# Two transposing transfers joined into one, and a planned order replaced by a written one, in an attention and feed-forward kernel

## The chip, the cores and the metric

The kernel runs on one core of a Trainium2 chip. A core has five engines that run side by side: PE (matrix products), DVE, ACT and POOL (element-wise work and copies) and SP, which here issues nearly all transfers. Each engine takes its instructions strictly in order and waits at an instruction until the semaphores that it names have been raised. The metric is the time of one execution on the device in microseconds (us). Before the change three runs gave 361.81, 362.72 and 363.73 us, a median of 362.72 us. One more execution was profiled; it took 361.35 us, and its trace spans 359.6 us from the first to the last instruction.

## The reference

There are 8 batches of 8 heads, 576 positions and a head size of 64. Each head has two attentions: one over positions pooled by four (144 of them), and one in a band of 7 positions around each query. Their sum, with the heads laid side by side (512 values for each of 4608 tokens), goes through a gated feed-forward.

```
q_d = q.reshape(B, H, Sd, factor, D).mean(axis=3)      # k_d and v_d likewise, factor = 4
out_up = np.repeat(sm_attn(q_d, k_d, v_d), factor, axis=2)
mask = np.abs(pos[:, None] - pos[None, :]) < factor
scores = np.where(mask, scale * np.matmul(q, k.transpose(0, 1, 3, 2)), -1000000000.0)
out_local = np.matmul(softmax(scores), v)
x = (out_up + out_local).transpose(0, 2, 1, 3).reshape(4608, 512)
out = (np.maximum(x @ w_gate, 0.0) * (x @ w_val)) @ w_out      # 512 -> 1536 -> 512
```

## The kernel before

**Pairs.** Two heads make a pair; there are 32 pairs, four for each batch. The work of pair p is a set of named operations that end in p. `lq`/`lk` load q and k. `cast` turns them into 16-bit values in the tile `c16`. The transposition puts the 64 features on partitions: for pairs 0 to 7 it is done on PE (`T`), from pair 8 on by a transposing transfer that SP issues (`dT`, line 1487), which reads 9 blocks of 128 x 128 from `c16` (`c` in the profile) and writes `tq`. `ev` copies `tq` into `qkT`, `pl` (DVE, line 1507) pools it, and `S` on PE makes the band scores (line 1518) and the pooled scores (line 1530). The band goes through `msk`, `mx`, `sub`, `exp`, `sm`, `rc`, `nrm` and two 32 x 32 transpositions on DVE (`tr0`, `tr1`). The pooled scores go through `dmx` (line 1592), `nb` (line 1595), three exponentials `exd0` to `exd2` (ACT, line 1605), `rcd` (line 1627) and `nrd` (POOL, line 1631) into the tile `wd`; then they too must be transposed: on PE (`W`) for pairs 0 to 7, and from pair 8 on by a second transposing transfer (`dW`, line 1654), 6 blocks from `wd` into `wT`. `V` on PE (lines 1731 and 1739) multiplies both by v. `od` (ACT) and `xa0`, `xa1` (DVE) add the two parts into the tile `xT`. Most tiles of a pair have three copies, used in turn by p mod 3.

**Feed-forward.** The tokens are taken in steps of mostly 512. `hg` and `hv` are the gate and value products (line 1798), 12 of each for a step; `rl` (ACT, line 1812) takes the positive part of the gate, and `gm` (DVE, line 1819) multiplies it by the value into `gT`. `y` is the output product of one block of 128 tokens (line 1864), in three parts of four matmuls; block 35, the last, has two halves of 256 columns (`y35_0`, `y35_1`, line 1843). ACT copies each block to an output buffer (`yc`, line 1873, and line 1851 for block 35) and SP stores it (`st`, line 1881, and 1854).

**Output buffers.** There are two, `y_sb` 0 and 1, each of two blocks. Blocks 28 and 29 take buffer 0, 30 and 31 buffer 1, 32 and 33 buffer 0, 34 and 35 buffer 1. Up to block 31 one store of 512 KB takes both blocks; blocks 32 to 34 are stored one by one (256 KB), and block 35 in two stores of 128 KB. A copy into a buffer waits until the store that last read this buffer has landed.

**Order.** A planner (`list_schedule`) gives every operation an estimated start, from estimated durations, priorities and a table of shifts by name (`RANKS`), chooses the engine where several can do it, and writes the operations out in that order. Ahead of a PE operation it also puts filler products of zeros (`emit_zeros`, line 1360, 128x512 each) where it foresees an idle PE in the first 34 us: 41 of them, beside 12 at the very start.

Of the kernel before, what the change touches and what calls it, by code (L numbers as in the profile page):

```python
# [21 lines left out]
class Op:  # L22
# [4 lines left out]
    def __init__(self, eng, dur, emit, deps=(), prio=0.0, need=None, key=None, free=(),  # L27
# [14 lines left out]
SEM = 0.12  # L42

MARGIN = 0.0


LATE, LATE_V = 0.0, 0.0
FETCH, FETCH_LATE, BUSY = 4.5, 4.0, 80.0

DMA_START = {SP: 0.8, POOL: 2.2}  # L50
RECEIPT = 1.2
W_AT = (14.0, 30.0, 34.0, 38.0)
WO_T0, WO_DT = 52.0, 6.0

# [3 lines left out]

FILL = 34.0
STOP = 0.3  # L60
LQ = (1.0, 1.3)
ISSUE = 0.75

RANKS = {
    -1054.5: (
        "lv2_25 "
    ),
    -699.5: (
        "od8 "
    ),  # L70
    -689: (
        "pl3 "
    ),
    -668.5: (
        "exd2_8 "
    ),
    -661: (
        "sub8 "
    ),
    -660: (  # L80
        "vd8 "
    ),
    -624: (
        "msk25 "
    ),
    -598.5: (
        "nb8 "
    ),
    -597: (
        "lv2_2 "  # L90
    ),
    -586: (
        "rc8 "
    ),
    -572: (
        "lq8 "
    ),
    -559.5: (
        "lv2_8 "
    ),  # L100
    -559: (
        "lk8 cast8 ev8 pl8 mx8 exd0_8 exd1_8 nrm8 nrd8 lv0_8 lv1_8 lv3_8 vc8 VP8 V8 xa0_8 "
        "xa1_8 "
    ),
    -558: (
        "msk8 "
    ),
    -548: (
        "rcd8 "
    ),  # L110
    -540.5: (
        "nb27 "
    ),
    -532: (
        "cast5 lv1_11 "
    ),
    -525: (
        "dT8 "
    ),
    -524: (  # L120
        "rc4 "
    ),
    -523.5: (
        "mx26 "
    ),
    -509: (
        "sm8 "
    ),
    -489: (
        "cast3 "  # L130
    ),
    -480: (
        "lv2_28 "
    ),
    -479.5: (
        "lv0_28 lv1_28 lv3_28 "
    ),
    -474: (
        "vs28 "
    ),  # L140
    -468: (
        "dW8 "
    ),
    -460.5: (
        "lv3_0 "
    ),
    -449: (
        "msk11 "
    ),
    -413: (  # L150
        "lv3_5 "
    ),
    -401.5: (
        "vd23 "
    ),
    -395.5: (
        "dmx7 "
    ),
    -372.5: (
        "cast26 "  # L160
    ),
    -364: (
        "od28 "
    ),
    -356.5: (
        "dT23 "
    ),
    -356: (
        "sub0 sub1 sub2 sub3 "
    ),  # L170
    -351: (
        "vd27 "
    ),
    -349.5: (
        "ev30 "
    ),
    -347.5: (
        "lv2_5 "
    ),
    -347: (  # L180
        "lv0_5 lv1_5 "
    ),
    -339: (
        "rcd9 "
    ),
    -338.5: (
        "sm7 "
    ),
    -338: (
        "nb11 "  # L190
    ),
    -333: (
        "exd2_28 "
    ),
    -325.5: (
        "sub28 "
    ),
    -324.5: (
        "vd28 "
    ),  # L200
    -322: (
        "dmx25 "
    ),
    -319.5: (
        "msk6 "
    ),
    -310.5: (
        "od0 od1 od2 od3 "
    ),
    -299: (  # L210
        "exp8 "
    ),
    -291: (
        "msk26 "
    ),
    -279: (
        "S8 "
    ),
    -271.5: (
        "vs15 "  # L220
    ),
    -265.5: (
        "vs23 "
    ),
    -263: (
        "nb28 "
    ),
    -254.5: (
        "lq0 "
    ),  # L230
    -251: (
        "mx30 "
    ),
    -250.5: (
        "rc28 "
    ),
    -249.5: (
        "exp12 "
    ),
    -249: (  # L240
        "msk12 "
    ),
    -247.5: (
        "nrd11 "
    ),
    -244.5: (
        "cast21 "
    ),
    -243: (
        "msk18 "  # L250
    ),
    -236.5: (
        "lq28 "
    ),
    -234: (
        "l4_28 "
    ),
    -233.5: (
        "dmx28 "
    ),  # L260
    -233: (
        "exp11 "
    ),
    -223.5: (
        "lk28 cast28 ev28 pl28 mx28 exp28 exd0_28 exd1_28 nrm28 nrd28 vc28 V28 xa0_28 "
        "xa1_28 "
    ),
    -221: (
        "ev11 "
    ),  # L270
    -220.5: (
        "exp9 "
    ),
    -212.5: (
        "rcd28 "
    ),
    -191: (
        "pl11 "
    ),
    -190: (  # L280
        "sub11 "
    ),
    -189.5: (
        "dT28 "
    ),
    -184.5: (
        "exd2_1 "
    ),
    -181: (
        "od23 "  # L290
    ),
    -176.5: (
        "exd2_5 od25 "
    ),
    -175: (
        "exd0_1 "
    ),
    -173.5: (
        "sm28 "
    ),  # L300
    -173: (
        "sm4 od26 "
    ),
    -169.5: (
        "od13 "
    ),
    -168: (
        "lv3_26 "
    ),
    -160.5: (  # L310
        "lv1_26 "
    ),
    -150: (
        "exd2_23 "
    ),
    -146.5: (
        "exd2_29 "
    ),
    -145.5: (
        "exd2_25 "  # L320
    ),
    -142.5: (
        "sub23 "
    ),
    -142: (
        "exd2_26 "
    ),
    -140.5: (
        "od9 od10 od11 od12 od14 od15 od16 od17 od19 od20 od21 od22 od24 od27 od29 od30 "
    ),  # L330
    -138.5: (
        "exd2_13 "
    ),
    -138: (
        "sub25 "
    ),
    -137: (
        "vd25 "
    ),
    -134.5: (  # L340
        "sub26 "
    ),
    -133.5: (
        "vd26 "
    ),
    -132.5: (
        "dW28 "
    ),
    -130: (
        "xa1_0 xa1_2 xa1_3 vd13 xa0_16 xa1_16 "  # L350
    ),
    -117.5: (
        "msk14 "
    ),
    -117: (
        "rc19 "
    ),
    -113: (
        "ev0_2 "
    ),  # L360
    -111: (
        "dmx20 "
    ),
    -110: (
        "dmx10 "
    ),
    -109.5: (
        "exd2_0 exd2_2 exd2_3 exd2_9 exd2_10 exd2_11 exd2_12 exd2_14 exd2_15 exd2_16 "
        "exd2_17 exd2_18 exd2_20 exd2_21 exd2_22 exd2_24 exd2_27 exd2_30 "
    ),  # L370
    -107: (
        "vd5 "
    ),
    -103: (
        "pl21 "
    ),
    -102: (
        "sub9 sub10 sub12 sub14 sub16 sub17 sub18 sub19 sub22 sub24 sub27 sub30 "
    ),
    -101.5: (  # L380
        "lv2_24 "
    ),
    -101: (
        "vd9 vd10 vd11 vd12 vd14 vd15 vd16 vd17 vd18 vd19 vd20 vd21 vd22 lv0_24 lv1_24 vd24 "
        "vd29 vd30 "
    ),
    -100.5: (
        "lk2 exd1_11 "
    ),
    -100: (  # L390
        "exd0_0 exd0_3 msk16 pl27 "
    ),
    -99.5: (
        "lq30 "
    ),
    -97.5: (
        "od5 "
    ),
    -96: (
        "nb18 "  # L400
    ),
    -94: (
        "rc5 "
    ),
    -88.5: (
        "lk0 "
    ),
    -87.5: (
        "nrd18 "
    ),  # L410
    -85: (
        "rcd0 rcd1 rcd2 "
    ),
    -80: (
        "nb23 "
    ),
    -75.5: (
        "nb25 "
    ),
    -75: (  # L420
        "exd1_1 "
    ),
    -72: (
        "nb26 "
    ),
    -71: (
        "mx18 "
    ),
    -70.5: (
        "xa1_23 "  # L430
    ),
    -69: (
        "msk20 "
    ),
    -68.5: (
        "nb13 "
    ),
    -68: (
        "lv3_24 "
    ),  # L440
    -67.5: (
# [1522 lines left out]
```

## Time and profile before

| what | value |
|---|---|
| median of three runs | 362.72 us |
| the profiled execution's own time | 361.35 us |
| its span | 359.6 us |
| busy time of PE, DVE, POOL and ACT | 350.2, 247.9, 204.5 and 202.8 us |
| granted PE clock, mean over the span | 0.999 |
| moved by transfers | 64.80 MB, 180 GB/s |

The busy time of an engine is the time in which at least one of its instructions runs; PE's instructions overlap, so this alone does not say that PE works at its peak. The chain of waits follows the work that ended last back to its cause at each step. A wait is time in which an engine stood still, with the instruction that released it.

### The profile page before, as it was taken

To read this page: it belongs to the slowest core of one execution; us is meant where nothing else is said; L and a number is where in the kernel's file an instruction comes from. 1 tells how busy PE (TensorE), PEld (TensorE's weight loads), DVE (VectorE), ACT (ScalarE), POOL (GpSimd) and SP (SyncE) were. 2 spreads that over 40 slices of the span, in tenths; PEclk is the share of its full clock that TensorE was granted. 3 is DMA by queue.
4 is the path that set the end of the run, shared out by engine and by line. 5 is a ranking of instruction groups with operands and counts; after the bars stand their busy time and mean duration, and the time that the engine had idled before them with its cause. 6 is when DMAs were issued, how large, how long until landed. Compare 5 with 4: busy or idle time off the path is not lost.

```text
span 359.6 us, 10503 instructions
## 1 busy us (share of the span) xinstructions
PE 350.2 (97%) x4241; PEld 182.5 (51%) x4241; DVE 247.9 (69%) x477; ACT 202.8 (56%) x481; POOL 204.5 (57%) x240
## 2 busy tenths in 40 slices
PE   7988999999999999999999999999999999999996
PEld 3554556445545554555555454544555454445554
DVE  4666998717988898978895986788988853223210
ACT  2477786537874757664566485768654533233222
POOL 7798475933387888684986369476898400000000
PEclk9999999999999999999999999999999999999999
DMA  7999999779999999999999898999994220011022
GB/s 190 201 272 255 195 227 292 110 185 152 259 232 212 228 280 167 278 224 264 198 230 233 190 271 182 215 261 224 217 237 65 47 93 26 0 60 59 0 75 102
DMA packets 122067, 64.80 MB, mean 180 GB/s; under 512 B 100386, under 2 KB 106402, under 8 KB 122018
## 3 DMA queue, kind: packets, MB, share of 16 engines
q1 hardware_dynamic: 116194, 59.41, 75.7%
q0 software_dynamic: 5824, 4.72, 8.6%
q8 instruction: 33, 0.54, 0.7%
q14 instruction: 16, 0.13, 0.1%
HBM read 47.59 MB, written 9.44 MB: 159 GB/s over the span
## 4 chain that ended last, share of the span: by engine, by line
PE 90%; POOL 5%; DMA 1%; issue 1%; DVE 1%; ACT 1%; POOLq 0%; SPq 0%
PE bank L1798 52%; PE bank L1864 25%; PE bank L1518 4%; PE bank L1731 2%; PE bank L1739 2%; DMA gT<-in_q_dram 1%; PE bank L1530 1%; POOL wo_sb L1330 1%; PE bank L1640 1%; PE bank L1695 1%; POOL vw L1352 1%; POOL wd L1631 1%; PE bank L1843 1%; POOL vw L1330 1%; POOL e L1615 1%
## 5 line engine op out<-in xcount | busy, mean ns | idle before, releaser
L1819 DVE TENSOR_TENSOR gT<-r,bank 128x512 f16<-128x512 f16 (+1 forms) x112 | 74.6, 666 | 64.1 <-PE bank L1798 59.9
L1798 PE MATMUL bank<-xT,wg_sb 128*128 128x512 f16 (+2 forms) x528 | 112.2, 341 | 0.0
L1798 PE MATMUL bank<-xT,wv_sb 128*128 128x512 f16 (+2 forms) x528 | 112.2, 341 | 0.0
L1812 ACT ACTIVATE r<-bank 128x512 f16<-128x512 f32 (+1 forms) x112 | 65.1, 583 | 67.2 <-PE bank L1798 62.9
L1864 PE MATMUL bank<-wo_sb,gT 128*128 128x512 f16 x420 | 96.6, 379 | 0.0
L1798 PEld LDWEIGHTS <-wg_sb 128*128 128x128 f16 x528 | 44.2, 98 | 45.5 <-issue 0.4
L1798 PEld LDWEIGHTS <-wv_sb 128*128 128x128 f16 x528 | 44.2, 98 | 44.6 <-issue 0.6
L1864 PEld LDWEIGHTS <-gT 128*128 128x128 f16 x420 | 39.8, 98 | 44.6 <-issue 0.4
L1873 ACT COPY y_sb<-bank 128x512 f32<-128x512 f32 x35 | 20.5, 586 | 52.0 <-PE bank L1864 49.6
L1330 POOL CAST vw<-vw 128x1536 f16<-128x1536 f32 x28 | 40.9, 1461 | 2.7 <-DMA vw<-in_v_dram 1.9
L1507 DVE TENSOR_REDUCE qkd<-qkT 128x288 f16<-128x1152 f16 x28 | 37.5, 1340 | 3.7 <-ACT qkT L1329 3.5
L1586 POOL TENSOR_TENSOR s_sb<-s_sb,mx 128x384 f32<-128x384 f32 x28 | 23.2, 831 | 28.8 <-DVE mx L1583 27.9
L1605 ACT ACTIVATE wd<-bank,nmb 128x144 f16<-128x144 f32 x96 | 35.6, 381 | 4.3 <-POOL nmb L1595 3.1
L1621 DVE STREAM_TRANSPOSE at<-e 64x384 f16<-64x384 f16 x64 | 36.4, 569 | 1.6 <-POOL e L1615 0.9
L1615 POOL TENSOR_TENSOR e<-e,rs 128x384 f16<-128x384 f16 x32 | 26.8, 839 | 14.7 <-DVE rs L1613 11.3
L1631 POOL TENSOR_TENSOR wd<-wd,rsd 128x432 f16<-128x432 f16 x32 | 29.0, 908 | 8.7 <-DVE rsd L1627 6.8
L1759 DVE TENSOR_TENSOR xT<-bank,od_sb 128x288 f16<-128x288 f32 (+2 forms) x68 | 26.7, 430 | 9.9 <-ACT od_sb L1750 9.8
L1717 POOL TENSOR_TENSOR vs<-v 104x512 f32<-104x512 f32 x20 | 25.3, 1267 | 2.1 <-DMA v<-in_v_dram 1.9
L1329 ACT COPY qkT<-tq 128x1152 f16<-128x1152 f16 x21 | 25.3, 1205 | 1.5 <-DMA tq<-c 1.4
L1518 PEld LDWEIGHTS <-qkT 64*32 64x32 f16 x1536 | 17.2, 90 | 11.9 <-issue 7.3
L1518 PE MATMUL bank<-qkT 64*32 64x32 f16 x1536 | 20.6, 180 | 1.0 <-DVE xT L1759 0.7
L1330 POOL CAST c<-qk 128x1152 f16<-128x1152 f32 x16 | 18.2, 1147 | 5.3 <-issue 3.9
(67 smaller groups left out, 347.5 us busy)
## 6 DMA issues: line engine op xcount, KB each, us to landing
vw<-in_v_dram SPq DMA_DIRECT2D x126, 96.0 KB, 4.7
out_dram<-y_sb SPq DMA_DIRECT2D x16, 512.0 KB, 3.8
qk<-in_q_dram SPq DMA_DIRECT2D x14, 576.0 KB, 4.9
qk<-in_k_dram SPq DMA_DIRECT2D x14, 576.0 KB, 6.9
v<-in_v_dram SPq DMA_DIRECT2D x10, 640.0 KB, 7.4
wv_sb<-in_moe_w_val_dram POOLq DMA_DIRECT2D x4, 384.0 KB, 10.0
wg_sb<-in_moe_w_gate_dram POOLq DMA_DIRECT2D x4, 384.0 KB, 9.4
wo_sb<-in_moe_w_out_dram POOLq DMA_DIRECT2D x4, 384.0 KB, 8.3
```

The costliest lines, as they stand in the source:

```text
L1330: return lambda o: engine[eng].tensor_copy(out=dst, in_=src(o))
L1507: nc.vector.tensor_reduce(out=qkd[S3].rearrange("p (x t) -> p x t", x=2), in_=qk_sums, axis=AX.X, op=ALU.add)
L1518: nc.tensor.matmul(out=scv[32 * c : 32 * c + 32, i, :], lhsT=cols(hh, q0 + step * 24 * blk, 32), rhs=cols(hh, k0 + step * (24 * blk - 3), 32),
L1605: exd.append(add(ACT, 0.37, lambda o, i=i: nc.scalar.activation(out=_sap(wd_, 0, 128, 256 * i + K0, kd_cols), in_=_sap(dview()[:, i, :], 0 ...
L1615: r["nrm"] = nrm = add_any(either(lambda o, e: e.tensor_tensor(out=e_, in0=e_, in1=bc12(rs[S3]), op=ALU.mult), (POOL, 0.84), (DVE, 0.5)), ...
L1621: tr.append(add(DVE, 0.575, lambda o, lo=lo: nc.vector.transpose(out=at2[S3][lo : lo + 64, :, lo // 2 : lo // 2 + 32], in_=e_[lo : lo + 64 ...
L1631: r["nrd"] = nrd = add_any(either(lambda o, e: e.tensor_tensor(out=_sap(wd_, 0, 128, K0, w3), in0=_sap(wd_, 0, 128, K0, w3), in1=_sap(rsd[ ...
L1759: nc.vector.tensor_tensor(out=xT[:, kk, (c1 + lo) % XR : (c1 + lo) % XR + hi - lo].rearrange("p (t f) -> p t f", f=4), in0=bank[V.banks[hf ...
L1798: nc.tensor.matmul(out=bank[(h or o).banks[0]][:, n * x : n * x + n], lhsT=w_sb[:, kk, bass.ts(jj, 128)], rhs=xT[:, kk, x_col(t0) : x_col( ...
L1812: rl = add(ACT, 0.17 + 0.00083 * n * m, lambda o: nc.scalar.activation(out=rt[:, 0 : n * m], in_=bank[f1.banks[0]][:, 0 : n * m], func=AF. ...
L1819: gm = add(DVE, 0.15 + 0.00104 * n * m, lambda o: nc.vector.tensor_tensor(out=gT[:, js[0] : js[0] + m, pos : pos + n], in0=rt[:, 0 : n * m ...
L1864: nc.tensor.matmul(out=bank[parts[0].banks[0]], lhsT=gT[:, jj, col : col + 128], rhs=wo_sb[:, jj, :], start=(jj == 0), stop=(jj == NJJ - 1))
```

## The change

The change has two parts.

**One transfer for two operands.** `wd` of a slot and `c16` of the same slot become two parts of one tile `cw` of 15 blocks, and `wT` and `tq` two parts of one tile `tqw`. Pairs p and p+3 use the same slot. From pair 8 on, `dW` of pair p now transposes all 15 blocks: the pooled weights of pair p and the cast q and k of pair p+3. The separate `dT` stays for pairs 8, 9 and 10 alone, and the last three `dW` (pairs 29 to 31), which have no pair p+3, stay at 6 blocks. So there are 3 + 21 + 3 = 27 transposing transfers in place of 48, of the same 360 blocks in all. The joined transfer waits for everything that the two waited for: `nrd` of pair p, `V` of pair p-3, `cast` of pair p+3 and `ev` of pair p.

**A written order.** The planner, its costs and its table go. A string of names gives the order of all operations, and each engine gets its own in this order. A name can be followed by the engine (`:P` POOL, `:A` ACT, `:D` DVE), by the PSUM banks behind a point, and by the number of fillers and their bank (`+6@1`; `+-1` means none).

```diff
-    for o in ops:
-        o.prio += SHIFT.get(o.name, 0.0)
-        o.after = ASK.get(o.name, o.after)
-    order = list_schedule(ops, {"F": [0, 1, 2, 3], "A": [4, 5, 6, 7]}, ...)
+    named = {o.name: o for o in ops}
...
+        for word in ORDER.split():
...
+            if fill:
+                n, _, b = fill.partition("@")
+                emit_zeros(int(b), int(n))
+            emit(o)
...
+ORDER = """
...
+ld_mask ld_sums lv0_1 lq2 T0.456+6@1 lv2_1 ev0_0:A lv1_1 cast1:P ev1_0:A lv3_1 pl0:D lv2_0
...
+gm4224_9 hv4224_10.3 rl4224_10 hg4224_11.2 gm4224_10 hv4224_11.0 rl4224_11 y30_0.1 gm4224_11 y30_1
+y30_2 y33_0.3 yc30 y33_1 y33_2 y35_0.2 yc33 st33 y35_1.0 y34_0.1 y34_1 y34_2 y31_0.3 y31_1 y31_2
+yc31 st31 yc34 yc35_0 st34 yc35_1 st35_0 st35_1
+"""
...
-    c16 = many(3, [128, 1152], FP16, "c16")
+    cw = many(3, [128, 15, 128], FP16, "cw")
+    c16 = [x[:, 0:9, :].rearrange("p a b -> p (a b)") for x in cw]
...
+    wd = [x[:, 9:15, :] for x in cw]
+    tqw = many(3, [128, 15, 128], FP16, "tqw")
+    tq = [x[:, 0:9, :] for x in tqw]
+    wT = [x[:, 9:15, :] for x in tqw]
...
+            if p - 3 < TD:
+                T = add(SP, 2.0, lambda o: nc.sync.dma_start(
+                    tq_, _sap(c_, 0, 128, 0, [[1, 1152]]), transpose=True),
+                    [cast, b3.get("ev")], prio=P + 11, xfer=1.2, name=f"dT{p}")
+            else:
+                T = b3["W"]
+                T.deps = list(T.deps) + [x for x in (cast, b3.get("ev")) if x is not None]
...
+            last = p + 3 >= NP
             r["W"] = evw = add(SP, 1.5, lambda o: nc.sync.dma_start(
-                wT[S3], _sap(wd_, 0, 128, 0, [[1, 768]]), transpose=True),
-                [nrd, b3.get("V")], prio=P + 30, xfer=0.8, name=f"dW{p}")
+                *((wT[S3], _sap(wd_, 0, 128, 0, [[1, 768]])) if last else
+                  (tqw[S3], _sap(cw[S3], 0, 128, 0, [[1, 1920]]))), transpose=True),
+                [nrd, b3.get("V")], prio=P + 30, xfer=0.8 if last else 1.3, name=f"dW{p}")
```

The matmuls are the same in number and shape but for the fillers: 25 of them stand in the program now (12 at the start, 6 ahead of `T0`, 3 ahead of `T1`, 4 ahead of `T3`) where 53 stood.

SP's queue in the middle of the program, before. `vw` and `v` are loads of v, `qk` of q and k; `tq<-c` is a `dT` and `wT<-wd` a `dW`.

```order
L1487 DMA_TRANSPOSE tq_107<-c_83 128x9x128 [waits DMAHW6_49,Pool_49]
L1654 DMA_TRANSPOSE wT_102<-wd_99 128x6x128 [waits DMAHW7_49,PE_49,Pool_49]
L1680 DMA vw_65<-in_v_dram 32x12x64 [waits DMAHW0_49]
L1487 DMA_TRANSPOSE tq_105<-c_81 128x9x128 [waits DMAHW1_49]
L1680 DMA vw_65<-in_v_dram 32x12x64 [waits DMAHW2_49]
L1710 DMA v_63<-in_v_dram 80x4x512 [waits DMAHW3_49,Pool_49]
L1430 DMA qk_62<-in_k_dram 64x4x576 [waits DMAHW4_49]
L1654 DMA_TRANSPOSE wT_103<-wd_100 128x6x128 [waits DMAHW5_49,PE_49,Pool_49]
```

The same stretch of SP's queue in the changed kernel:

```order
L694 DMA vw_65<-in_v_dram 32x12x64 [waits DMAHW2_49]
L667 DMA_TRANSPOSE tqw_101<-cw_83 128x15x128 [waits PE_49,DMAHW3_49,Activation_49,Pool_49]
L436 DMA qk_62<-in_k_dram 64x4x576 [waits DMAHW4_49]
L436 DMA qk_62<-in_q_dram 64x4x576 [waits DMAHW5_49]
L694 DMA vw_65<-in_v_dram 32x12x64 [waits DMAHW6_49]
L694 DMA vw_65<-in_v_dram 32x12x64 [waits DMAHW7_49]
L667 DMA_TRANSPOSE tqw_99<-cw_81 128x15x128 [waits DMAHW0_49,PE_49,Pool_49]
```

Two transfers of 15 blocks stand where four of 9 and 6 stood, and each waits for the engines of both.

The end of ACT's queue, before: `r` is the positive part of the last gate products, `y_sb` the copies of the output blocks 31, 32, 33, 34 and the two halves of 35.

```order
L1873 COPY y_sb_72<-bank_141 128x512 [waits PE_49]
L1812 ACTIVATE r_78<-bank_138 128x384 [waits DVE_49,PE_49]
L1812 ACTIVATE r_79<-bank_140 128x384 [waits DVE_49,PE_49]
L1812 ACTIVATE r_80<-bank_138 128x384 [waits PE_49,Activation_49]
L1873 COPY y_sb_71<-bank_140 128x512 [waits DMAHW1_49,PE_49]
L1873 COPY y_sb_71<-bank_141 128x512 [waits DVE_49,PE_49]
L1873 COPY y_sb_72<-bank_138 128x512 [waits DMAHW2_49,PE_49]
L1851 COPY y_sb_72<-bank_139 128x256 [waits DVE_49,PE_49]
L1851 COPY y_sb_72<-bank_140 128x256 [waits PE_49]
```

The end of ACT's queue in the changed kernel, with the copies of blocks 30, 33, 31, 34 and the halves of 35:

```order
L826 ACTIVATE r_80<-bank_134 128x384 [waits PE_49,Activation_49]
L887 COPY y_sb_72<-bank_133 128x512 [waits DMAHW3_49,PE_49]
L887 COPY y_sb_71<-bank_135 128x512 [waits DVE_49,PE_49]
L887 COPY y_sb_72<-bank_135 128x512 [waits PE_49]
L887 COPY y_sb_72<-bank_133 128x512 [waits DMAHW7_49,Activation_49]
L865 COPY y_sb_72<-bank_134 128x256 [waits Activation_49]
L865 COPY y_sb_72<-bank_132 128x256 [waits DVE_49]
```

The copy of block 31 has moved from ahead of the last gate products to behind block 33, and the three copies behind it go into the same buffer, `y_sb_72`; the first of them waits for a transfer (`DMAHW7`).

The end of SP's queue in the changed kernel, the stores of blocks 28 and 29, 32, 33, 30 and 31, 34, and the halves of 35:

```order
L895 DMA out_dram<-y_sb_71 128x2x512 [waits DMAHW4_49,Activation_49]
L895 DMA out_dram<-y_sb_71 128x512 [waits DMAHW5_49,Activation_49]
L895 DMA out_dram<-y_sb_71 128x512 [waits DMAHW6_49,Activation_49]
L895 DMA out_dram<-y_sb_72 128x2x512 [waits Activation_49]
L895 DMA out_dram<-y_sb_72 128x512 [waits DMAHW0_49,Activation_49]
L868 DMA out_dram<-y_sb_72 128x256 [waits DMAHW1_49,Activation_49]
L868 DMA out_dram<-y_sb_72 128x256 [waits DMAHW2_49,Activation_49]
```

The queue semaphores are taken in turn, 0 to 7, so the fourth row, the 512 KB store of blocks 30 and 31, is the transfer that `DMAHW7` tells of. On PE the last products stood in the order of the blocks, 32, 33, 34, 35; now they stand 30, 33, 35, 34, 31.

1267 lines of the change are left out of this document (143 added, 1124 removed).

## The prediction

> **What bounds the kernel now.** I read the page's busy times, then its chain of waits by engine, then busy times in stretches cut where the work changes.
>
> ```profile
> PE 350.2 (97%) x4241; PEld 182.5 (51%) x4241; DVE 247.9 (69%) x477; ACT 202.8 (56%) x481; POOL 204.5 (57%) x240
> ...
> PE 90%; POOL 5%; DMA 1%; issue 1%; DVE 1%; ACT 1%; POOLq 0%; SPq 0%
> ```
>
> ```profile
> core 0: us, PE busy (x) PEld busy (x) DVE busy (x) ACT busy (x) POOL busy (x), PEclk, DMA share, GB/s
> 20.00:32.00 12.00, 9.67 (x189) 6.20 (x182) 8.68 (x21) 7.93 (x26) 10.85 (x13) 1.00 1.16 285
> 32.00:41.00 9.00, 8.17 (x134) 5.04 (x134) 6.14 (x10) 7.87 (x12) 5.39 (x7) 1.00 1.31 201
> 41.00:275.00 234.00, 233.92 (x3121) 120.95 (x3120) 191.55 (x368) 149.69 (x359) 166.18 (x190) 1.00 1.06 220
> 275.00:293.00 18.00, 18.00 (x182) 9.19 (x181) 13.91 (x30) 8.91 (x26) 6.80 (x9) 1.00 0.14 29
> 293.00:356.60 63.60, 63.52 (x330) 32.11 (x328) 15.68 (x26) 19.31 (x36) 0.00 (x0) 1.00 0.14 53
> ```
>
> From 41 us to its last product PE is busy 233.92 + 18.00 + 63.52 = 315.4 of 315.6 us, at a granted clock of 1.00. A busy PE can still be slow, so its pace was checked in the chain of waits, in order of time:
>
> ```profile
> 294.27 10.36 PE bank L1798 x48
> 304.63 2.59 PE bank L1864 x12
> ```
>
> 48 wide products take 10.36 us and 12 take 2.59 us: 216 ns each both times. So the kernel has three parts: a start-up of about 41 us in which PE waits for others, 315 us in which nothing but PE's own work counts, and an end behind the last product. PE's products stay the same in number and shape, so the middle can hardly get shorter. A reordering can lose there, win in the start-up, or change the end.
>
> **The joined transfer: worth nothing by itself.** The transposing transfers by tile, with their issue on SP, who waited for them, and the time to landing:
>
> ```profile
> L1487 SPq DMA_TRANSPOSE tq<-c x24: 1242/1402/5262, 70.2 to 266.5; - x24
>   ACT qkT L1329: 1.4, 2
> DMA to landing us min/median/max: 3.3/4.2/6.8
> L1654 SPq DMA_TRANSPOSE wT<-wd x24: 1209/1281/3917, 90.2 to 285.2; - x24
> DMA to landing us min/median/max: 2.7/4.8/8.3
> ```
>
> The change saves 21 transfers, 21 x 1.28 = 27 us of SP's queue. But nothing on PE waited for a transposed tile; the waits above are ACT's. Between 41 and 293 us all this lies beside a PE that never stops. I take 0 for the saving.
>
> The price is the coupling: scores of pair p+3 now need the softmax of pair p. The links, from the groups by line:
>
> ```profile
> L1592 DVE TENSOR_REDUCE nmx<-bank 128x3 f32<-128x432 f32 x32 | 18.9, 593 | 1.4 <-PE bank L1530 1.3
> L1595 POOL TENSOR_SCALAR nmb<-nmx 128x3 f32<-128x3 f32 x32 | 7.3, 230 | 9.8 <-DVE nmx L1592 9.6
> L1605 ACT ACTIVATE wd<-bank,nmb 128x144 f16<-128x144 f32 x96 | 35.6, 381 | 4.3 <-POOL nmb L1595 3.1 <-DMA wT<-wd 1.2
> L1605 ACT ACTIVATION_READ_ACCUMULATOR wd<-bank,nmb 128x1 f32 x96 | 19.8, 206 | 0.0
> L1627 DVE RECIPROCAL rsd<-smd 128x6 f32<-128x6 f32 x32 | 5.6, 176 | 2.4 <-ACT wd L1605 1.9
> L1631 POOL TENSOR_TENSOR wd<-wd,rsd 128x432 f16<-128x432 f16 x32 | 29.0, 908 | 8.7 <-DVE rsd L1627 6.8 <-ACT e L1589 1.7 <-ACT r L1812 0.2
> L1329 ACT COPY qkT<-tq 128x1152 f16<-128x1152 f16 x21 | 25.3, 1205 | 1.5 <-DMA tq<-c 1.4
> L1507 DVE TENSOR_REDUCE qkd<-qkT 128x288 f16<-128x1152 f16 x28 | 37.5, 1340 | 3.7 <-ACT qkT L1329 3.5
> ```
>
> From the scores to a finished `wd`: 0.59 + 0.23 + 3 x (0.38 + 0.21) + 0.18 + 0.91 = 3.7 us. A transfer of 15 blocks was never run. Least times of 2.7 us for 6 blocks and 3.3 for 9 give 0.2 us a block, so at least 4.5 us; the upper end is the longest seen plus 9 more blocks, 8.3 + 1.8 = 10.1. I take 6, near the medians of 4.2 and 4.8 plus the extra blocks. Then `ev` and `pl`, 1.2 + 1.3. In all 12.2 us, or 16.3 at the upper end. The written order must hold that much PE work between `S` of a pair and `S` of the pair three on. I counted the shortest case, pairs 12 to 15: 9 thirds of a block and 8 gate or value products, 17 x 0.86 = 14.7 us, with two other `S` and three `V` of about 0.6, 17.7 in all. The cover holds, by 1.4 us even at the upper end. From `S30` to `V30` stand 6 gate and value products, 6 thirds of a block and one `S`, 11.0 us, against 3.7 plus a 6-block transfer of 2.7 to 8.3: 6.4 to 12.0, so a stall of 0 to 1.0 us, and as much for `V31`.
>
> The other tight place is where scores stand close together, `S9` and `S8` with some 3 us between their starts now. Before, the same density stood here:
>
> ```profile
> 236.83 0.27 PE bank L1518 x28
> 238.38 0.27 PE bank L1518 x28
> ```
>
> 1.55 us apart, and PE did not stop. Here, though, the pooled-value products of pairs 8 to 10 follow directly and need PSUM banks that ACT must first empty; one exponential (0.59) or copy (0.6) too late is a stall of that size. Stalls in the middle together: 0 to 3 us. I take **+0.8**, near the low end, because the nearest rows show none.
>
> **The fillers.** 28 fillers go. The first and third rows are two that go; behind each is what followed it:
>
> ```profile
> 28.13 1.46 PE L1360 MATMUL bank<-r 128*128 128x512 f16 x6
> 30.02 0.31 PE L1731 MATMUL bank<-at,vw 128*128 128x48 f16 x6 [0.28 <-ACT vdz L1329]
> ...
> 32.16 0.38 PE L1360 MATMUL bank<-r 128*128 128x512 f16 x1
> 32.38 0.81 PE L1798 MATMUL bank<-xT,wg_sb 128*128 128x512 f16 x3
> ```
>
> The six at 28.13 us end before ACT releases the product at 30.02: in a gap, free. The one at 32.16 stands right ahead of the first gate product and delays it by 32.38 - 32.16 = 0.22 us. Bounds: no loss, and a gain up to 1.0 us if ACT and POOL let PE close more of the 0.83 us that it is idle in 32 to 41 us. I take **-0.3**.
>
> **The end: the term that decides.** Before, it looks like this in the chain of waits, with ACT's copy and a late store of 512 KB; the row of digits is the transfers' share in 40 slices of 325 to 340 us:
>
> ```profile
> 353.90 2.63 PE bank L1843 x24
> 356.54 0.02 issue
> 356.56 0.37 ACT y_sb L1851
> ```
>
> ```profile
> 353.94 0.58 ACT L1873 COPY y_sb<-bank 128x512 f32<-128x512 f32 x1 [2.00 <-PE bank L1864]
> ```
>
> ```profile
> 329.90 24.98 SPq L1881 DMA_DIRECT2D out_dram<-y_sb  x5
> ```
>
> ```profile
> DMA  0000000000000005999100000000000000000000
> ```
>
> ```profile
> L1881 SPq DMA_DIRECT2D out_dram<-y_sb x19: 332/405/1415, 77.7 to 354.5; - x19
> ...
> DMA to landing us min/median/max: 2.0/3.3/4.3
> ```
>
> PE's last product ends at 353.90 + 2.63 = 356.53; one copy of 0.37 us and the last store follow, and the span closes at 359.6: 3.07 us behind PE, of which 359.6 - 356.93 = 2.67 behind the last copy. In the changed kernel PE's last product is block 31. Behind it stand in line: its copy (0.58); the store of blocks 30 and 31; then, since block 34 goes into the same buffer and its copy waits for that store's landing, the copies of 34 (0.58) and of the halves of 35 (2 x 0.37), all of whose products were done long before; then the 2.67. The store at 329.90 moves data until slice 19 ends, 332.5, so I take 2.7 us; bounds 2.0 and 4.3 from the row. Handovers, about 0.1. Sum: 0.58 + 2.7 + 0.58 + 0.74 + 2.67 + 0.1 = 7.4, less 3.07: **+4.3**. Three stores, 512 KB together, now follow within 0.74 us, and 512 KB needs some 1.5 us of transfer, so the last queues for 0 to 0.6: I add 0.3. The term is **+4.6**, bounds 3.6 and 6.5.
>
> **Sum.** -0.3 + 0.8 + 4.6 = +5.1 us. Against the profiled execution, 361.35, that gives 366.4; it lay 1.37 us under the median of 362.72, from which it would be 367.8. I forecast the middle, **367.1 us**.
>
> [...] All stretches above show a granted clock of 1.00, with fillers in the gaps. Here is the largest gap that opens:
>
> ```profile
> 14.97 0.67 PE L1460 MATMUL bank<-ident_sb,wo_sb 96*128 96x96 f16 x12 [0.28 <-DVE s_sb L1576]
> 18.70 0.47 PE L1518 MATMUL bank<-qkT 64*32 64x32 f16 x42 [0.21 <-ACT qkT L1329]
> ```
>
> From 15.64 to 18.70 us, 3.1 us, one short product is left. Should the clock halve there and stay so up to 41 us, the 8.17 us of PE work in 32 to 41 would double at worst; from 0 to 8.2, I take 3 us. [...] No row of this trace shows the clock fall before the end, so it stays a rival.
>
> **Rivals.**
> - *Late transposes.* If 15 blocks land later than 10 us while transfers are busy (share 1.06 in 41 to 275 us), `S` of pair p+3 waits, some 21 times at most. A landing at 13 us would cost 13 - 10.1 - 1.4 = 1.5 us at the tightest pairs; with two or three such, 4 us on top: 371. Against it: most pairs are 20 us and more apart. Chance 0.10.
> - *The clock halves in the start-up*: +3, 370 us. Chance 0.05.
> - *The fillers were on the path.* All 28 at 216 ns are 6.0 us. Then PE ends 6.0 earlier: 361.35 - 6.0 + 0.8 + 4.6 = 360.7, not slower than before. It decides from 25 fillers on, where 25 x 0.216 equals 5.4. Against it: the waits for ACT and POOL behind the gaps. Chance 0.08.
> - *The end does not do what its order says*: PE's last block comes early enough, or the store lands unseen, so that the end costs nothing: -0.3 + 0.8, 361.9 to 363.2. For it only that I read an order, not a run. Chance 0.07.
>
> **How the numbers follow.** The forecast has 0.70. Its own bounds run from 361.35 - 1.0 + 3.6 = 364.0 to 362.72 + 3 + 6.5 = 372.2; both extremes at the upper end at once are unlikely, so I cut it to 371.5. The two slower rivals lie mostly within; about 0.2 is left out. About 0.5% (1.8 us) is what a measurement of this kernel can tell from no change. Slower: 0.70 + 0.10 + 0.05 = 0.85. The last two rivals give 0.15, most of it within the bound: 0.11, and 0.04 for faster.
>
> **What would show it.** Right: PE's last product ends within 356 to 360 us, as a block of line 878; then an ACT copy, a gap of nearly 3 us that a store releases, three copies in a row, and the span ends 7 to 8 us behind PE. Behind 41 us PE has no wait over 1 us. Wrong: ACT's last copies follow PE without a gap; PE waits for `qkT` or `tqw` in the middle; a clock under 1.00 ahead of 41 us; or a first gate product well before 32 us.

## The result, and the profile after

| | before | changed |
|---|---|---|
| median, us (lowest to highest of four executions) | 362.52 (361.81 to 363.73) | 368.71 (366.89 to 368.92) |
| the profiled execution's own time | 361.35 | 368.86 |
| its span | 359.6 | 367.0 |
| end of PE's last product | 356.53 | 358.86 |
| span behind it | 3.07 | 8.13 |

The ratio is 1.0156 with a 95% interval from 1.0113 to 1.0199: slower by 6.2 us between the medians, by 7.5 us between the two profiled executions. Of the 7.4 us that the span grew, 5.1 lie behind PE's last product and 2.3 ahead of it. The two traces differ by 1.3 us more than the medians, because the profiled execution before lay 1.2 us under its median; so the split of the traces overstates the loss somewhere by about that much, and only one execution of each kernel has a trace to look at.

The page of the changed kernel, with the lines for busy time and for the shares of the chain of waits:

```profile
PE 347.1 (95%) x4213; PEld 180.9 (49%) x4213; DVE 248.3 (68%) x479; ACT 205.6 (56%) x483; POOL 200.4 (55%) x236
...
PE 77%; DMA 11%; DVE 4%; POOL 3%; ACT 2%; issue 1%; SPq 1%; ACTq 0%; POOLq 0%; DVEq 0%
```

PE is busy for 3.1 us less in a span that is 7.4 us longer (28 fillers of 216 ns would be 6.0 us less; products at half clock, below, take some of it back: the changed kernel's four 128x512 fillers between 17.04 and 23.86 us took 627 ns each, the 36 of before between 8 and 34 us, at full clock, 379), and its share of the chain falls from 90% to 77%. Where the loss stands is seen in the end of the timeline (start, duration, engine and line; in brackets the idle time before it and what ended it):

```profile
353.52 5.34 PE L878 MATMUL bank<-wo_sb,gT 128*128 128x512 f16 x24
358.90 0.59 ACT L887 COPY y_sb<-bank 128x512 f32<-128x512 f32 x1 [7.21 <-PE bank L878]
362.38 0.59 ACT L887 COPY y_sb<-bank 128x512 f32<-128x512 f32 x1 [2.89 <-DMA out_dram<-y_sb]
362.86 0.65 ACT L865 COPY y_sb<-bank 128x256 f32<-128x256 f32 x2
363.41 0.87 SPq L868 DMA_DIRECT2D out_dram<-y_sb  x2
```

The chain of waits over the same place:

```profile
353.68 5.20 PE bank L878 x24
358.88 0.02 issue
358.90 0.59 ACT y_sb L887
359.50 0.02 issue
359.51 2.79 DMA out_dram<-y_sb
```

After PE's last product, ACT copies block 31, then stands still for 2.89 us until the store of blocks 30 and 31 has landed, then copies block 34 and the halves of 35, which PE had finished before block 31. Only then can the last stores start.

The other 2.3 us: busy time of each engine in stretches of the changed kernel (PE's first, and PEclk, the granted clock, third from the right), first four stretches of 3.41 us in the start-up, then the middle:

```profile
10.21:13.62 3.41, 2.91 (x146) 2.27 (x146) 1.35 (x3) 1.19 (x2) 1.02 (x2) 1.00 1.24 194
13.62:17.04 3.42, 1.39 (x28) 1.19 (x25) 3.35 (x8) 1.50 (x5) 3.25 (x6) 1.00 1.13 168
17.04:20.45 3.41, 1.61 (x59) 0.71 (x62) 2.96 (x9) 3.20 (x14) 3.41 (x4) 0.50 1.19 214
20.45:23.86 3.41, 3.09 (x30) 1.33 (x28) 2.12 (x5) 1.59 (x5) 2.82 (x4) 0.50 1.26 238
...
41.00:275.00 234.00, 232.53 (x3051) 119.74 (x3050) 187.71 (x361) 152.37 (x360) 155.80 (x179) 1.00 1.03 220
```

Here the clock fell to half for 6.8 us, which the profiled execution before does not show ahead of its end. In the middle PE is idle for 1.47 us where it was idle for 0.08 (234.00 less 233.92). PE's waits between 41 and 359 us, with the total, the number and the longest:

```profile
PE bank L530 <- issue: 0.7, 2, 0.5
PE bank L753 <- DMA tqw<-cw: 0.6, 1, 0.6
PE bank L542 <- ACT cw L617: 0.2, 1, 0.2
```

What the start-up lost by its end is seen at the pair scores of pair 5, first in the kernel before, then in the changed one:

```profile
37.79 0.20 PE L1518 MATMUL bank<-qkT 64*32 64x32 f16 x4 [0.66 <-DVE xT L1759]
```

```profile
38.31 0.20 PE L530 MATMUL bank<-qkT 64*32 64x32 f16 x4 [0.67 <-DVE xT L773]
```

This is 0.52 us later. The remaining 1.8 us arise behind it.

### The profile page after: what moved, and what is told of

Its sections match the earlier page's. It is cut to its first block, busy times and chain, and to the rows that moved or that the text cites. A ratio compares the mean times of both kernels' runs of the same rounds, so it can differ in the third digit from the quotient of the medians.

```text
span 367.0 us, 10393 instructions
## 1 busy us (share of the span) xinstructions
PE 347.1 (95%) x4213; PEld 180.9 (49%) x4213; DVE 248.3 (68%) x479; ACT 205.6 (56%) x483; POOL 200.4 (55%) x236
## 4 chain that ended last, share of the span: by engine, by line
PE 77%; DMA 11%; DVE 4%; POOL 3%; ACT 2%; issue 1%; SPq 1%; ACTq 0%; POOLq 0%; DVEq 0%
PE bank L812 47%; PE bank L878 19%; DMA tqw<-cw 7%; PE bank L530 3%; DMA vw<-in_v_dram 2%; PE bank L745 2%; PE bank L753 2%; DMA gT<-in_q_dram 1%; POOL cw L643 1%; PE bank L542 1%; PE bank L652 1%; DVE at L633 1%; PE bank L709 1%; DMA out_dram<-y_sb 1%; DVE vw L358 1%
## 5 line engine op out<-in xcount | busy, mean ns | idle before, releaser
L878 PE MATMUL bank<-wo_sb,gT 128*128 128x512 f16 x420 | 98.0, 379 | 0.0
L336 POOL CAST vw<-vw 128x1536 f16<-128x1536 f32 x27 | 39.4, 1462 | 12.0 <-PE bank L745 9.8
L617 ACT ACTIVATE cw<-bank,nmb 128x144 f16<-128x144 f32 x96 | 35.9, 382 | 8.9 <-POOL nmb L607 8.6
L643 POOL TENSOR_TENSOR cw<-cw,rsd 128x432 f16<-128x432 f16 x32 | 29.4, 920 | 5.4 <-DVE rsd L639 5.0
L598 POOL TENSOR_TENSOR s_sb<-s_sb,mx 128x384 f32<-128x384 f32 x27 | 22.4, 831 | 15.9 <-DVE mx L595 15.8
L335 ACT COPY qkT<-tqw 128x1152 f16<-128x1152 f16 x20 | 24.0, 1201 | 5.3 <-DMA tqw<-cw 5.2
L530 PEld LDWEIGHTS <-qkT 64*32 64x32 f16 x1536 | 17.2, 90 | 15.8 <-issue 10.1
L336 POOL CAST cw<-qk 128x1152 f16<-128x1152 f32 x14 | 16.0, 1146 | 14.0 <-issue 7.0
```

Of the source, the lines that this page charges most:

```text
L336: return lambda o: engine[eng].tensor_copy(out=dst, in_=src(o))
L530: nc.tensor.matmul(out=scv[32 * c : 32 * c + 32, i, :], lhsT=cols(hh, q0 + step * 24 * blk, 32), rhs=cols(hh, k0 + step * (24 * blk - 3), 32),
L617: exd.append(add(ACT, 0.37, lambda o, i=i: nc.scalar.activation(out=_sap(wd_, 0, 128, 256 * i + K0, kd_cols), in_=_sap(dview()[:, i, :], 0 ...
L643: r["nrd"] = nrd = add_any(either(lambda o, e: e.tensor_tensor(out=_sap(wd_, 0, 128, K0, w3), in0=_sap(wd_, 0, 128, K0, w3), in1=_sap(rsd[ ...
L878: nc.tensor.matmul(out=bank[parts[0].banks[0]], lhsT=gT[:, jj, col : col + 128], rhs=wo_sb[:, jj, :], start=(jj == 0), stop=(jj == NJJ - 1))
```

## The experiments

**The theory**: the end's order costs about 5 us, the missing fillers about 1 through the clock, and the joined transfer together with the order written for it nothing that can be measured. **Rivals**: the loss sits in the coupling of the joined transfer; or the fillers are of no account. Times are medians. The ratios are to the kernel before on the same chip, and versions that were run at different times are compared by their ratios.

**1. The end alone reordered.** Block 31 goes back ahead of the last blocks, so that they stand 30, 31, 33, 34, 35 on PE, ACT and SP.

```diff
-y30_2 y33_0.3 yc30 y33_1 y33_2 y35_0.2 yc33 st33 y35_1.0 y34_0.1 y34_1 y34_2 y31_0.3 y31_1 y31_2
-yc31 st31 yc34 yc35_0 st34 yc35_1 st35_0 st35_1
+y30_2 y31_0.3 yc30 y31_1 y31_2 y33_0.2 yc31 st31 y33_1 y33_2 y34_0.0 yc33 st33 y34_1 y34_2 y35_0.1
+yc34 st34 y35_1.3 yc35_0 st35_0 yc35_1 st35_1
```

> The changed kernel with only its end reordered: the products of block 31 right behind those of block 30, then 33, 34 and the halves of 35 last, and their copies and stores in the same order. Theory (the copy of block 34 waits for the store of blocks 30 and 31): PE's last product ends where it did, near 358.9 us, the span closes 3.1 us behind it and not 8.1, so the time is 5.0 us less, about 363.7. Rival (the end is long for another reason, such as a slow last store): the span still closes 8 us behind PE, 368.7. Second rival (PE loses what the end wins, since blocks 30 and 31 now follow each other): PE's end moves later by more than 1 us.

Measured: 363.25 us, ratio 1.0009 (0.9988 to 1.0030). The chain of waits at the end of this version, and ACT's last two copies in its timeline:

```profile
355.63 2.63 PE bank L857 x24
358.26 0.02 issue
358.28 0.37 ACT y_sb L865
```

```profile
357.03 0.37 ACT L865 COPY y_sb<-bank 128x256 f32<-128x256 f32 x1 [0.74 <-PE bank L857]
358.28 0.37 ACT L865 COPY y_sb<-bank 128x256 f32<-128x256 f32 x1 [0.88 <-PE bank L857]
```

The copies follow PE one by one, and the span of 361.6 closes 3.4 us behind PE, in place of 8.1. Nearly the whole difference from before is gone with two lines of the order: the end is the loss.

**2. The fillers back.** 41 fillers at the nine places of the kernel before; the changed end stays.

```diff
-T0.456+6@1  T1.123+3@0  T2.230       Sl2.1+-1@5  T3.674+4@1  W1.3+-1@1  V2.12+-1@1  W3.4+-1@4  hg0_0a.0+-1@0
+T0.456+5@1  T1.123+8@0  T2.230+3@5   Sl2.1+10@5  T3.674+3@1  W1.3+4@1   V2.12+6@1   W3.4+1@4   hg0_0a.0+1@0
```

> The changed kernel with the 41 fillers of before at the same nine places in place of its 13. Theory (the clock was halved from 17.0 to 23.9 us because PE was too idle): the granted clock stays at 1.00 from its first rise on, the first gate product starts at 32.4 us in place of 32.7, PE's steady work begins 0.5 us earlier, and the time falls by 0.3 to 0.8 us, to about 368.1. Rival (the clock falls at that place for another reason): it falls again near 17 us and nothing moves. Second rival (the fillers take PE time that others need): the first gate product starts later than 32.7 us.

Measured: 367.0 us, ratio 1.0123 (1.0101 to 1.0144). That is 1.7 us under the changed kernel by the medians and 1.2 by the ratios (0.0033 x 362.5), more than expected, though the intervals of the two ratios overlap; in the traces PE's last product ends 1.68 us earlier, at 357.18. The granted clock in its start-up:

```profile
17.82:21.24 3.42, 2.04 (x70) 1.00 (x69) 3.31 (x9) 2.62 (x11) 3.42 (x4) 1.00 1.23 240
21.24:24.65 3.41, 3.34 (x29) 2.07 (x29) 1.65 (x6) 2.09 (x8) 3.41 (x6) 0.50 1.27 225
```

One stretch is at half clock in place of two. The theory had said none: the fillers did not remove the fall altogether.

**3. A third output buffer** for blocks 34 and 35, so that their copies wait for no store; the order stays.

```diff
-    y_sb = many(2, [128, 2, DM], FP32, "y_sb")
+    y_sb = many(3, [128, 2, DM], FP32, "y_sb")
-        two = y_sb[n_y // 2 % 2]
+        two = y_sb[2 if n_y >= 34 else n_y // 2 % 2]
```

> The changed kernel with a third output buffer that blocks 34 and 35 use, in the same order. It takes away the wait for the store and leaves block 31 last on PE and its copy ahead of those of 34 and 35. Theory: ACT's four last copies follow each other, 0.59 + 0.59 + 2 x 0.37, and the span closes 4.8 to 5.3 us behind PE, so 2.8 to 3.3 us less than 368.7: about 365.7. If the queue of copies and not the wait were the cost, it would stay at 368.7; if the order of the copies cost nothing, it would fall by 5 us to 363.7.

Measured: 366.52 us, ratio 1.0113 (1.0074 to 1.0153); the span closes 6.1 us behind PE's last product, above what was expected. ACT's copies, and then the stretches behind PE with the transfers' busy share and rate in the last two columns:

```profile
358.30 1.07 ACT L887 COPY y_sb<-bank 128x512 f32<-128x512 f32 x2 [7.21 <-PE bank L878]
359.26 0.67 ACT L865 COPY y_sb<-bank 128x256 f32<-128x256 f32 x2
```

```profile
358.27:359.95 1.68, 0.00 (x0) 0.00 (x0) 0.00 (x0) 1.63 (x4) 0.00 (x0) 1.00 0.07 28
359.95:362.90 2.95, 0.00 (x0) 0.00 (x0) 0.00 (x0) 0.00 (x0) 0.00 (x0) 0.93 0.94 340
362.90:364.40 1.50, 0.00 (x0) 0.00 (x0) 0.00 (x0) 0.00 (x0) 0.00 (x0) 0.50 0.00 0
```

The wait is gone, and 2.0 us of the 5.1 with it. The other 3 stay, because four copies (1.6 us) still begin only when PE has ended, and then 340 GB/s x 2.95 us = 1.0 MB of stores go out at once, with the transfers 94% busy. So the wait for the store is the smaller part. The larger one comes of block 31 being last: the finished blocks 34 and 35 stand behind it in ACT's queue, and the 512 KB store of blocks 30 and 31 cannot start before it either. No run separates these two.

**4. The join undone, both transfers at the place of the joined one.** The order is otherwise the changed kernel's; `dT14` is one of 21 names put in.

```diff
-            if p - 3 < TD:
+            if True:
-            last = p + 3 >= NP
+            last = True
-... pl12 vc12:A y4_2 vd12:P dW11 xa0_9 ...
+... pl12 vc12:A y4_2 vd12:P dT14 dW11 xa0_9 ...
```

> The changed kernel with the joined transfer undone: at each of the 21 places two transfers, 9 blocks of q and k of pair p+3 and then 6 blocks of pooled weights of pair p, one right behind the other. The order is otherwise the same. Theory (joining is worth nothing on PE's path, and costs a late landing at one or two places): the wait of 0.6 us for the transposed tile near 165 us changes by less than 1 us either way, PE's end stays within 1 us of 358.9, time 368 to 369. Rival (joining relieves SP's queue and the transfers, and the order needs it): loads and transposes fall behind, PE waits for them in the middle, and the time rises by 2 us or more, over 370.7.

Measured: 370.36 us, ratio 1.0207 (1.0180 to 1.0234), so 1.7 us above the changed kernel by the medians, with intervals that still overlap a little. PE's waits between 41 and 365 us (line 619 is `V`):

```profile
PE bank L619 <- DMA tqw<-cw: 3.5, 3, 1.8
PE bank L678 <- ACT y_sb L753: 2.3, 1, 2.3
```

The profiled execution was the longest of five, 374.35 us, so these totals are high; but the first wait is the one that the joined version has for 0.6 us. In this order the join seems to be worth something; the time alone does not show it beyond the noise.

**5. The join undone, and `dT` issued right behind its operands** (the cast of its pair and `ev` of the pair three before), not at the place of `dW`.

```diff
-... V9.56 xa1_8 cast14:P y6_1 od9 rc11 pl12 vc12:A y4_2 vd12:P dT14 dW11 xa0_9 ...
+... V9.56 xa1_8 cast14:P dT14 y6_1 od9 rc11 pl12 vc12:A y4_2 vd12:P dW11 xa0_9 ...
```

> Changed kernel with the joined transfer split into two as in the kernel before, the one of the pooled weights issued right behind the cast and the evictions of its pair, the one of the cast q and k at the place of the joined one. Theory (two issues and their shares of SP's queue and of the DMA engines are what the order lacks room for; the run with both at one place gave 370.36): still 370 to 371, with PE waiting over 1 us in the middle for a transposing transfer. Rival (the two-transfer run was late only because both stood at the late place): 368.0 to 369.0, no PE wait of over 1 us behind 41 us.

(This text names the two transfers the other way round: the edit moves the one of the cast q and k, `dT`, and leaves that of the pooled weights, `dW`, where the joined one stood.)

Measured: 375.57 us, ratio 1.0359 (1.0317 to 1.0402), worse than both expected. PE's waits:

```profile
PE bank L619 <- DMA tqw<-cw: 2.6, 3, 1.2
PE bank L619 <- POOL vw L202: 1.6, 1, 1.6
PE bank L678 <- ACT y_sb L753: 1.0, 1, 1.0
```

Issuing `dT` early does not mend it: its late place was not the cause. The first row is `V` waiting for `dW`, which had not moved. The profiled execution's mean granted clock was 0.977 over 373.9 us, so some 17 us at half by an estimate from these two, with 1.00 between 41 and 275 us; what of it lay ahead of PE's end is in the time too. The second row is new: a cast of v was late. Between 41 and 275 us SP stood still ahead of `dT` (line 360) for 54.7 us in all, where in run 4 it did for 38.6, and the loads of v stand behind it in the queue; that is the likely reason, but no run took it alone.

**6. The kernel before, its planner kept, with only the transfers joined.** The edits to the tiles and transfers are those of the change; nothing else is.

> Kernel before, with its planner still setting the order, and only the transfers joined (pooled weights of pair p with the cast q and k of pair p+3). Theory (the join alone frees SP's queue, on which PE does not wait in that order): 362.0 to 363.2, no difference from before. Rival (the join couples two producers, and the planner's order is late for it): 364 to 367, with PE waits on the transfer or on its producers in the middle.

Measured: 379.77 us, ratio 1.0467 (1.0428 to 1.0506). PE's waits between 41 and 375 us (line 1747 is `V`, 1739 its product with the band's weights, 1536 the pooled scores):

```profile
PE bank L1747 <- DMA tqw<-cw: 6.4, 5, 2.3
PE bank L1739 <- DVE at L1627: 1.9, 1, 1.9
PE bank L1536 <- ACT cw L1611: 1.4, 1, 1.4
```

and its middle:

```profile
41.00:275.00 234.00, 222.30 (x2901) 113.79 (x2900) 181.28 (x343) 144.88 (x339) 147.60 (x170) 0.98 0.93 207
```

PE is idle for 11.7 us where it was idle for 0.08, and the clock fell to half there for 10.2 us in all (a mean of 0.98 in this row), so the products themselves took longer too: PE's busy time over the whole span is 356.5 us, against 350.2. The coupling is real, and dear where the order makes no room for it: the rival's mechanism, at four times the most that it said.

**7. Fillers of the changed kernel in the kernel before**: 6, 3 and 4 of them ahead of `T0`, `T1` and `T3`, and none elsewhere.

```diff
+                o.fill = {'T0': 6, 'T1': 3, 'T3': 4}.get(o.name, 0)
                 if o.fill and spare:
```

> Kernel before, with the fillers at the three places and in the numbers (6, 3, 4) of the changed kernel instead of 41 at nine. Theory (the missing fillers let the clock fall in start-up, for one window of 3.4 us or two): a granted clock of 0.5 for 3.4 to 6.8 us between 10 and 41 us, PE's last product 0.7 to 1.7 us later, 363.3 to 364.3. Rival (fillers are worth nothing in the order of before): clock 1.0 from 7 us on and 362.2 to 362.9.

Measured: 368.34 us, ratio 1.0147 (1.0111 to 1.0184). The clock fell, to half for 10.2 us between 16 and 37 us (means of 0.82, 0.86 and 0.81 in 10 to 20, 20 to 32 and 32 to 41 us), where the theory had 3.4 to 6.8, and the time is 4 us over its range. In the trace one place holds most of that. PE's waits behind 41 us:

```profile
PE bank L1518 <- issue: 3.4, 2, 3.2
```

At 101 us PE stood still for 3.2 us with no releaser in the trace, and one more stretch at half clock followed at 105 us (a mean of 0.99 from 105 to 275). During 8 us around it the transfer queue that the profile calls `instruction` shows two packets with 2.0% of the transfer engines' time, where the kernel before has one with 0.8%; what held PE up is not shown. The same scores, those of pair 11, wait in this way for 0.5 us in the changed kernel, at 103 us. Whether the missing fillers caused the long wait, and whether every execution has it, stays open.

**8. Both repairs at once**: the end of run 1 and the fillers of run 2.

> Changed kernel with the end reordered (as in the run at 363.25) and the 41 fillers of before at their nine places (as in the run at 367.0). Theory (end costs 5.1, fillers 1.7 and the two are independent): PE's last product ends near 357.2, 3.2 to 3.4 us behind it, the time 361.5 to 362.3. Rival (the fillers' 1.7 was only the position of the clock's drops): 363.2 to 363.8, as without them.

Measured: 362.44 us, ratio 0.9988 (0.9965 to 1.0012), and PE's last product ends at 357.13, as the theory expected; the time is 0.1 us above its range and well below the rival's. The middle:

```profile
41.00:275.00 234.00, 233.67 (x3063) 120.77 (x3062) 190.48 (x366) 153.49 (x362) 156.44 (x179) 1.00 1.01 220
```

Joined transfers and the written order keep PE as busy here as the kernel before (233.92). With runs 1 and 2 this makes a table of ratios:

| | 13 fillers | 41 fillers |
|---|---|---|
| end as changed | 1.0156 | 1.0123 |
| end reordered | 1.0009 | 0.9988 |

The end is worth 0.0147 and 0.0135 (5.3 and 4.9 us), the fillers 0.0033 and 0.0021 (1.2 and 0.8 us, each less than its own uncertainty of about 0.005 and 0.003), and what is left of the change, the join in its written order, nothing that can be measured.

**9. Five more fillers in run 8**, where PE is idle between 18 and 21 us, to hold the clock.

```diff
-... VP0.5+-1@5 pl2:A rcd0 mx2 Sd2.0+-1@4 vd0:A lq6 sub2 dmx2 cast3:P exp2 VP1.2+-1@2 ...
+... VP0.5+2@5 pl2:A rcd0 mx2 Sd2.0+1@4 vd0:A lq6 sub2 dmx2 cast3:P exp2 VP1.2+2@2 ...
```

> The run at 362.44 (end reordered, 41 fillers of before) with five more fillers where PE is idle between 18 and 21 us: 2 ahead of the first pooled q and k product of pair 0, 1 and 2 at the two places behind. Theory (the granted clock of a stretch of 3.41 us is set by PE's busy share in the stretch before: in the traces so far every stretch at full clock under 0.50 busy was followed by a half one, every one over 0.67 by a full one, and 18.35 to 21.76 there had 0.65): clock 1.00 from 8 us to PE's end, PE's last product 0.3 to 0.8 us earlier than 357.13, time 361.7 to 362.2. Rival (the clock falls for another reason, the DMA load or the wait itself): a drop between 15 and 30 us again, 362.4 to 363.2.

Measured: 362.89 us, ratio 1.0022 (1.0003 to 1.0042). (`VP0`, called a product of q and k in what was expected, pools v.) The stretch at stake in run 8 (two rows), then in this one:

```profile
18.35:21.76 3.41, 2.21 (x75) 1.09 (x74) 3.32 (x8) 2.75 (x12) 3.41 (x4) 1.00 1.23 240
21.76:25.17 3.41, 3.41 (x33) 2.68 (x32) 1.64 (x6) 1.84 (x10) 3.41 (x5) 0.50 1.23 244
```

```profile
17.58:21.00 3.42, 3.08 (x75) 1.23 (x72) 3.31 (x8) 2.89 (x12) 3.41 (x3) 1.00 1.25 241
21.00:24.41 3.41, 3.41 (x54) 1.96 (x43) 1.55 (x5) 2.37 (x10) 3.18 (x4) 1.00 1.25 232
```

The clock stayed at 1.00 up to the end, as the theory said. The time did not follow: in the profiled execution PE then waited 1.0 us for a `gT` and 0.5 at an issue in the middle, and its last product ended at 358.10, later than in run 8. The pair of runs cannot price these 3.4 us, though: in run 8 the mean granted clock was 0.994 in the traced execution and 0.995 in one more, but 1.000 in the other ten of twelve. Most of run 8 thus held its clock already, and its trace shows the exception.

**10. Ten fillers alone in the changed kernel**, ahead of the band mask's product of pair 2, where PE stands still from 16.1 to 18.7 us.

```diff
-... exd1_0 Sl2.1+-1@5 tr1_1 ...
+... exd1_0 Sl2.1+10@5 tr1_1 ...
```

> Changed kernel with only ten fillers more, ahead of the log-product of pair 2, where PE stands still between 16.1 and 18.7 us and where the kernel before has ten. Theory (clock follows the busy share of the stretch before): no stretch under 0.50 between 13 and 21 us, so no 6.8 us at half clock there (one stretch of 3.4 us may stay, at 0.5 to 0.67), PE's last product 0.6 to 1.2 us earlier than 358.86, end unchanged at 8.1, time 367.0 to 368.0. Rival (all 41 fillers are needed): 6.8 us or more at half clock, 368.3 to 369.0.

Measured: 368.01 us, ratio 1.0163 (1.0141 to 1.0185), between the two ranges. The stretch from 14.51 is now 2.83 us busy and keeps its clock, and PE's last product ends at 357.92, 0.94 earlier; but the clock fell later, from 21.34 and from 31.57 us, for 6.8 us in all (a mean of 0.92 over the first 41 us), which the rival had said:

```profile
17.92:21.34 3.42, 2.02 (x74) 1.13 (x74) 3.33 (x8) 2.38 (x9) 3.42 (x4) 1.00 1.24 232
21.34:24.75 3.41, 3.41 (x29) 2.42 (x28) 1.63 (x6) 1.55 (x8) 3.41 (x5) 0.50 1.21 256
28.16:31.57 3.41, 1.75 (x39) 1.26 (x38) 3.00 (x9) 2.51 (x12) 2.36 (x4) 1.00 1.10 332
```

Between 13 and 21 us no stretch was under 0.50 and the 6.8 us there are gone, as the theory said, with one half stretch behind them, which it allowed; the second, behind a stretch 0.51 busy, it did not foresee. For the time the run decides nothing, since its ratio is that of the changed kernel.

## Why the prediction was right, point by point

- **The end, +4.6: right, and it decides.** Measured 5.1. By its own parts: the copy of 31 took 0.59 (0.58 said), the store 2.79 (2.7), the three copies 362.38 to 363.52, or 1.14 (1.32), and 3.48 passed behind the last copy (2.67 and 0.3 for the queue). The last part was the one sized too small. Run 1 removes the term by undoing this part alone. Run 3 corrects the picture in one point: the wait for the buffer, which the prediction made its centre, accounts for 2.0 of the 5.1; without it the four late copies and the 1 MB of stores behind them still cost 3.
- **The middle, +0.8, bounds 0 to 3: within its bounds, not confirmed as a cost.** PE's idle time between 41 and 275 us grew by 1.4 us in the profiled execution; in runs 1, 2 and 8, with the same middle, it is 0.33, which is 0.25 more than before. The places named, `S9` with `S8` and `V30` with `V31`, are not those that waited.
- **The joined transfer, "worth nothing by itself": wrong as it stood.** The working looked for waits on a transposed tile in the trace of before, found none, and took 0. That is the saving against the order of before. In the changed order the two transfers apart took 1.7 us more (run 4, at the edge of the noise), and in the planner's order the join costs 17 us (run 6). So neither part has a price of its own; only join and order together come out at nothing (run 8). The 27 us that the join was to free on SP's queue did not come in the changed kernel: the working took it that a joined transfer occupies SP no longer than one of the two that it replaces, but the median is 2.84 us, where the two had 1.28 and 1.40. Added up, the transposing transfers occupy SP for 83.1 us in the changed kernel's trace and 80.0 before (75.4 in run 8). The landings, 8.9 us at most, stayed under the 10.1 that the prediction allowed:

```profile
L667 SPq DMA_TRANSPOSE tqw<-cw x24: 1212/2840/5346, 90.7 to 294.8; - x24
...
DMA to landing us min/median/max: 2.7/5.0/8.9
```

- **The fillers, -0.3: wrong in sign, as far as the runs tell.** They were seen as work in gaps that could only be free or in the way. PE's clock went with them too: without 28 of them it fell for 6.8 us, with them back for 3.4 (run 2). Putting them back gave 0.8 and 1.2 us by the ratios (runs 1, 2 and 8), each within its noise; in the traces PE's last product then ended 1.1 us earlier (run 8 against run 1) and 1.7 earlier (run 2 against the changed kernel, 1.1 of them waits in the middle). All point one way, but the price is not settled.
- **The clock**, a rival with a chance of 0.05: it happened, and with it one of the prediction's own signs of being wrong. It cost about 1 us, not 3, so the sum bore it. The 1 us is an estimate from the pairs above and from run 1 alone, where one stretch at half is 0.0047 of the mean granted clock: the five executions at 0.991 took 361.54 to 363.39 us, the three at 0.986 363.23 to 363.39, the two at 0.981 363.71 and 364.70. Run 3 has the same order; runs 4 and 5 do not. In the stretch from 13.62 to 17.04 us PE was busy for 1.39 of 3.42 us and its longest idle time was 0.91 us, and the clock fell at its end.
- **The other rivals.** Late transposes came once in the changed kernel, for 0.6 us, another of the signs named, but far from the 4 us of the rival; run 6 shows them where the order is not made for them. Fillers on the path: refuted, since with fewer of them the start-up was later (0.52 us at pair 5), not 6 us earlier. An end without cost: refuted.

Of the 7.4 us in the profiled spans, 5.1 are thus the end, 0.5 the start-up up to pair 5, and 1.8 what follows up to PE's last product; of the last, 1.5 stand in the table of PE's waits above, and no run tells what the rest is. The mechanism of the end was foreseen and shown. The nearness of the sum beside it, +5.1 against 6.2 between the medians, is in part luck: +0.8 for stalls and -0.3 for fillers were both off, and together they stand in for a clock that was not in the sum.

## What to carry to other kernels

Read the last operations of each in-order queue against the time at which their operands are ready: a finished block behind an unfinished one costs its copy and its store at the end, where nothing hides them; here that was 5.1 us. A transfer that waits for two producers has no price by itself; it has one in an order (here 17 us in the planner's and nothing that can be measured in the written one), so try it with the order that makes room for it and without. Filler products in a gap look free to remove, but look at what PE's busy share in that stretch becomes without them: here one of 0.41 was followed by 6.8 us at half clock.

## What the runs showed of the hardware

In the trace of before, the record of the granted clock begins at 4.04 us with 1.00 (128x512 fillers took 618 ns each ahead of it, and 379 between 8 and 34 us) and stays there for 354.99 us, 104 times 3.413 us. In that of the changed kernel it begins at 6.80 us and is at 1.00 for 10.24 us, at 0.50 for 6.83 and at 1.00 again for 337.92: 3, 2 and 99 times 3.413 us. With the time cut into these stretches, and where PE still works in the whole of the next, the trace of before has 102 stretches at full clock; the least busy of them has a share of 0.68, and full clock followed each. The trace of the changed kernel has 100: half clock followed the one with a share of 0.41, and full clock the other 99, of 0.68 and more. Stretches of these two and of the runs, by PE's busy share:

| execution | from, us | PE busy, us | share | clock in the next |
|---|---|---|---|---|
| changed | 13.62 | 1.39 | 0.41 | 0.50 |
| run 10 | 28.16 | 1.75 | 0.51 | 0.50 |
| run 10 | 17.92 | 2.02 | 0.59 | 0.50 |
| run 2 | 17.82 | 2.04 | 0.60 | 0.50 |
| run 8 | 18.35 | 2.21 | 0.65 | 0.50 |
| before | 17.69 | 2.34 | 0.68 | 1.00 |
| run 10 | 14.51 | 2.83 | 0.83 | 1.00 |
| run 9 | 17.58 | 3.08 | 0.90 | 1.00 |

The row of before is the one of its start-up:

```profile
17.69:21.11 3.42, 2.34 (x76) 1.14 (x74) 3.31 (x9) 2.61 (x11) 3.42 (x4) 1.00 1.24 238
```

Against run 8, run 9 moved such a stretch from 0.65 to 0.90, and the clock stayed. One stretch does not fit the order of the table: in run 2 the one from 355.74 us, in which PE's work ended, was 0.42 busy, and by an estimate full clock followed it. The mean granted clock of 0.992 over 365.3 us leaves 5.5 to 6.2 us at half in all, and the stretch in the start-up with the time from 362.57 us on already makes 6.1. So whether the busy share alone sets the clock is not shown, nor what would hold for another kernel.

The same program did not always get the same clock: of 47 executions of the kernel before, six have a mean of 0.994 or 0.995, which is one stretch at half (0.0047), and the rest 0.999 or 1.000. That this explains the spread of the times is not shown; the six took 361.82 to 365.18 us, and the others spread as widely.
